# Attention, a rational-gate layer and four experts in one kernel: elementwise work of the front on GpSimd, another load order, and the last expert's products with the operands exchanged

## The chip, the cores and the metric

The kernel runs on one core of a Trainium2 chip. Five engines work side by side, each in the order of its own instructions: TensorE (PE, with its weight loads as PEld), VectorE (DVE), ScalarE (ACT), GpSimd (POOL) and SyncE (SP), which here only issues transfers. They wait for each other by semaphores. The metric is device time in microseconds (us); a smaller time is better.

## The reference, cut to what matters

Three layers follow each other. All is float32; NB = 4 batches, NH = 8 heads, S = 768 steps, D = 48.

```python
# 1: gated linear attention, per batch and head
f = 1 / (1 + exp(-f_logit))
state = f[t] * state + outer(k[t], v[t]);  y[t] = q[t] @ state
# 2: x: (3072, 384) from y;  w_in (384, 2048), w_out (2048, 384)
h = x @ w_in
g = (a0 + a1*h + a2*h**2 + a3*h**3) / (1 + |b0|*|h| + |b1|*h**2 + 1e-6)
x = g @ w_out
# 3: four experts, F = 1024
p = domain_probs / (domain_probs.sum(-1) + 1e-9)
out += p[:, e:e+1] * (relu(x @ w1[e]) @ w2[e])
```

## The kernel before

**Tiling.** The 768 steps are cut into six chunks of 128 steps (`c`), and a chunk holds the four batches' tokens side by side: 4 x 128 = 512 tokens. In a chunk the attention is made by block `(c, b)`, one for a batch. A block loads `f`, `k`, `q` (`Block.load`, 256 KB each) and `v` (`load_v`, 320 KB), takes `exp` and 1 + exp (`w`), multiplies along the steps by four scans (`scans`, result `g`), takes 1/g by logarithm, exponential and one Newton step (`inverse`, `newton1`, `newton2`), scales k by g (`k_hat`) and q by 1/g (`q_hat`), and then needs TensorE for the scores (`scores`), the transposed k (`k_t`, copied out by `k_copy`), the masked product with v (`masked`, `intra`) and the state's update (`update`, `finish`). `x_hi` copies the block's rows to x.

**The front.** Chunk 0 has nothing beside it. `Att.first(s, ...)` is called for s = 0 to 4 and writes out by hand the work of block s (`new`), block s - 1 (`old`) and the exponential of block s + 1 (`nxt`). In the same calls the weights of layer 2 come in as 64-bit numbers (`fetch`: two transfers of 768 KB, `raw`) and are turned into float32 by `conv(i, stage)`: two ScalarE instructions, a shift and a bit operation on VectorE, and one integer addition; the result `wf` is stored to DRAM (`w1s`). `conv` 0 falls into s = 1, 1 into s = 2, 2 and 3 into s = 3. In this kernel the addition of 0 to 3 and `k_hat` and `q_hat` of chunk 0 are VectorE's, the addition of 4 to 15 and `k_hat` and `q_hat` of later chunks GpSimd's. `warm` issues small products that nothing needs. The first product of layer 2 (`fill_in`, L880) waits for `x_hi` of block 3. Behind it come 6 chunks of layers 2 and 3, woven with the attention of the next chunk.

**The steady part.** Matrices and inputs of the later products are split into a high and a low part (`float32r`, one pass over TensorE), and each product is three: high by high, low by high, high by low. `mm_in` gives a 128 x 512 tile of h (nine instructions), `relu` its two parts, `mm_out` adds to three accumulators of 128 x 512 (nine instructions; rows are model columns, columns tokens). Products of chunk 0 in layer 2 are plain float32 (L880, L887), which takes two instructions each.

**The end.** When an expert is done, `evac2` multiplies the accumulators by the tokens' probabilities, spread over the rows (`pb`), and GpSimd adds them to `o`. For the last expert of the last chunk `end` does it on VectorE in six pairs of instructions, and then `write_out` turns `o` by twelve transposes on TensorE, copies by ScalarE and stores.

**Transfers.** SP issues nearly all transfers, in the order of the program. The program has eight semaphores for them, used in turn, so that the issue of a transfer waits until the one eight places before it (ScalarE's four first ones counted) has landed. It also waits until its target buffer is free: `f`, `k`, `q` and `v` have two buffers each.

Of the kernel before, what the change touches and what calls it, by code (L numbers as in the profile page):

```python
# [19 lines left out]
C = 128  # L20
# [379 lines left out]
class Block:  # L400
# [42 lines left out]
    def k_hat(self):  # L443
        k = self.k[0:PR]
        eng = self.nc.gpsimd if self.c else self.nc.vector
        eng.tensor_tensor(out=k, in0=k, in1=self.g[0:PR], op=ALU.mult)

# [10 lines left out]
    def q_hat(self):  # L458
        q = self.q[0:PR]
        eng = self.nc.gpsimd if self.c else self.nc.vector  # L460
        eng.tensor_tensor(out=q, in0=q, in1=self.i[0:PR], op=ALU.mult)

# [90 lines left out]
class Att:  # L553
# [24 lines left out]
    def start(self, fetch):  # L578
        nc = self.tc.nc
        for b in range(NB):  # L580
            nc.gpsimd.memset(self.st[b], 0.0)
        for b in range(2):
            blk = self.blocks[0, b] = Block(self, 0, b)
            for i in (2, 1, 0):
                blk.load(i)
            blk.load_v()
        for _ in range(3):
            fetch()

# [5 lines left out]

    def first(self, s, conv):

        new, old, nxt = (self.blocks.get((0, b)) for b in (s, s - 1, s + 1))
        rs = range(NP)
        if s == 0:  # L600
            new.exp()
            self.warm(WARM[0])
        if old:
            old.k_copy()
        if new:
            new.w()
            new.scans()
            new.inverse()
            new.k_hat()
        if nxt:  # L610
            nxt.exp()
# [29 lines left out]
        if old and s + 1 < NB:  # L641
            self.blocks[0, s + 1].load_v()

    def loads(self, v):
# [44 lines left out]
def fused(ctx, tc, aps, consts, gm, big, dp, prep, flag_op):  # L689
# [7 lines left out]
    banks = [pp.tile([128, 512], F32, name=f"bank{i}") for i in range(8)]  # L697
    acc, hb, h1 = banks[0:3], banks[3:5], banks[5]

    def pool(name, bufs):  # L700
# [27 lines left out]
    def conv(i, stage):  # L728
# [11 lines left out]
        else:  # L740
            nc.vector.tensor_scalar(pi, pi, 3, None, ALU.logical_shift_left)
            nc.vector.scalar_tensor_tensor(out=pi, in0=hi, scalar=-2 ** 31, in1=pi, op0=ALU.bitwise_and, op1=ALU.bitwise_or)
            w1f[i] = wp.tile([128, SW], F32, tag="w", name="wf")
            eng = nc.vector if CONV1[i] < NB - 6 else nc.gpsimd
            eng.tensor_tensor(out=w1f[i].bitcast(I32), in0=pi, in1=m, op=ALU.add)
            late.append(partial(nc.sync.dma_start, out=w1s[i], in_=w1f[i]))
# [99 lines left out]
    def mm_out(pairs, start, stop):  # L846
        for m in range(3):
            o = slice(m * 128, (m + 1) * 128)
            n, last = 0, 3 * len(pairs) - 1
            for (wh, wl), (gh, gl) in pairs:  # L850
                for a, b in ((wh, gh), (wl, gh), (wh, gl)):
                    nc.tensor.matmul(acc[m], a[:, o], b, start=(start and n == 0), stop=(stop and n == last))  # L852
                    n += 1
                    fill_step()

    def run_bounds(v):

        return (v % NJ2 == 0 or v in groups), ((v + 1) % NJ2 == 0 or v + 1 in groups)

    def emit(item):  # L860
# [9 lines left out]
        elif kind == "out2":  # L870
            mm_out([(ts[0], act2.pop(what))], *run_bounds(what))
        else:
# [137 lines left out]
    def write_out(c, b, bank):  # L1010
        for m in range(3):
            nc.tensor.transpose(bank[:, m * C:(m + 1) * C], o[c][:, m, b * C:(b + 1) * C], ident)
        if c < NCH - 1:
            t = osp.tile([128, DM], F32, tag="os", name="os")
        else:
            if b == 0:
                last.append(sp.tile([128, 3, 512], F32, tag="s1", name="os"))
            t = last[0].rearrange("p m t -> p (m t)")[:, b * DM:(b + 1) * DM]
        nc.scalar.copy(out=t, in_=bank[:, 0:DM])
# [14 lines left out]
    for v in range(-FILL - 6, LAST + 1):  # L1034
# [4 lines left out]
        if tau + 6 <= NB:  # L1039
            att.first(tau + 6, conv_ops(tau) if tau + 6 < NB else [[], []])  # L1040
        run_late()
# [254 lines left out]
```

## Time and profile before

| | us |
|---|---|
| median of 3 runs | 1397.06 (1396.53 to 1398.14) |
| the profiled execution, whole | 1395.27 |
| its span, first to last instruction | 1393.5 |
| PE, DVE, ACT, POOL busy | 1335.1, 889.1, 665.3, 290.5 |

The profile is one execution. What it shows lies in its span; some 1.8 us around it belong to the execution too. Busy shares are means over a front (up to 54 us), in which TensorE waits for the others, a long middle part, in which they wait for TensorE, and an end of some ten microseconds.

### The profile page before, as it was taken

Reading aid. Unit: us, or ns where it says so; the run is one execution under the profiler, and the core shown is the slowest. Engines: PE = TensorE matmul, PEld = TensorE weight load, DVE = VectorE, ACT = ScalarE, POOL = GpSimd, SP = SyncE. Lnnn points to the kernel's source line nnn. Section 1 sums busy time; section 2 is a strip of 40 time slices with the busy share of each in tenths; the row PEclk is TensorE's granted clock in tenths of the full one; section 3 lists DMA queues with packets and bytes.
Section 4 is the critical chain, followed back from the end, with each engine's and each line's share of the span. In section 5 each row is a group of like instructions: output and inputs, shape, how many; then the busy total and the mean of one; then the engine's idle time right before and its main releaser. Section 6 shows DMA issues by size and latency. Waiting matters only on the chain.

```text
span 1393.5 us, 19540 instructions
## 1 busy us (share of the span) xinstructions
PE 1335.1 (96%) x7134; PEld 1060.5 (76%) x7134; DVE 889.1 (64%) x1375; ACT 665.3 (48%) x1152; POOL 290.5 (21%) x257
## 2 busy tenths in 40 slices
PE   4799999899899999999999999999999999999997
PEld 4544787677678888877888877888888888888886
DVE  5899747697947666757666676566675556552222
ACT  3688437676626535534554435454454453431111
POOL 0133554566530010112001111001111001111010
PEclk8999999999999999999999999999999999999998
DMA  7546876667875656656755647566557566657660
GB/s 271 201 172 213 282 257 222 216 219 254 311 267 184 213 181 200 217 180 220 223 190 182 213 159 264 194 205 215 188 175 254 179 209 193 193 193 240 193 186 26
DMA packets 115704, 291.03 MB, mean 209 GB/s; under 512 B 13104, under 2 KB 28816, under 8 KB 114832
## 3 DMA queue, kind: packets, MB, share of 16 engines
q1 hardware_dynamic: 115024, 289.51, 62.8%
q8 instruction: 59, 0.97, 0.3%
q14 instruction: 45, 0.37, 0.1%
q10 hardware_dynamic: 576, 0.18, 0.1%
HBM read 240.83 MB, written 48.81 MB: 208 GB/s over the span
## 4 chain that ended last, share of the span: by engine, by line
PE 79%; DVE 13%; ACT 3%; DMA 2%; issue 1%; POOL 0%; SPq 0%; ACTq 0%; DVEq 0%; POOLq 0%
PE bank L852 36%; PE bank L842 33%; PE bank L887 3%; PE bank L880 3%; PE bank L489 2%; PE bank L465 1%; DVE q L916 1%; DVE g L435 1%; DMA f<-in_qkf_dram 1%; DVE q L925 1%; DVE y L935 1%; DVE y L937 1%; DVE q L911 1%; DVE q L913 1%; DVE gl L951 1%
## 5 line engine op out<-in xcount | busy, mean ns | idle before, releaser
L842 PE MATMUL bank<-x,w 128*128 128x512 f32 x2448 | 604.5, 394 | 11.3 <-DVE gl L951 9.1
L842 PEld LDWEIGHTS bank<-x,w 128*128 128x128 f32 x2448 | 457.3, 189 | 107.9 <-DVE gl L951 11.6
L852 PE MATMUL bank<-gh,w 128*128 128x512 f32 x1632 | 516.8, 396 | 6.6 <-DVE t L987 6.6
L852 PEld LDWEIGHTS bank<-gh,w 128*128 128x128 f32 x1632 | 302.8, 189 | 73.3 <-DVE t L987 7.4
L852 PE MATMUL bank<-gl,w 128*128 128x512 f32 x816 | 320.6, 393 | 0.0
L951 DVE SCALAR_TENSOR_TENSOR gl<-bank,gh 128x512 fp32r<-128x512 f32 x192 | 131.4, 685 | 153.0 <-ACT gh L950 152.5
L988 POOL TENSOR_TENSOR o<-o,t 128x512 f32<-128x512 f32 x69 | 89.0, 1319 | 549.4 <-DVE t L987 549.4
L852 PEld LDWEIGHTS bank<-gl,w 128*128 128x128 f32 x816 | 153.9, 189 | 33.1
L950 ACT ACTIVATE gh<-bank 128x512 fp32r<-128x512 f32 x192 | 113.6, 593 | 130.7 <-PE bank L842 130.7
L916 DVE SCALAR_TENSOR_TENSOR q<-q,sc,r 128x512 f32<-128x512 f32 x80 | 62.4, 780 | 152.3 <-ACT r L901 152.3
L799 POOL TENSOR_TENSOR w<-rawbuf,w 128x384 fp32r<-128x384 f32 x96 | 108.0, 1151 | 93.5 <-ACT w L798 77.5
L927 ACT CAST gh<-q 128x512 fp32r<-128x512 f32 x80 | 49.2, 615 | 159.0 <-DVE q L925 158.9
L896 ACT COPY h<-bank 128x512 f32<-128x512 f32 x80 | 46.8, 585 | 127.7 <-PE bank L842 127.2
L1005 DVE TENSOR_TENSOR s<-s,bank 128x512 f32<-128x512 f32 x45 | 30.6, 681 | 74.1 <-PE bank L852 74.1
L942 DVE TENSOR_TENSOR gl<-q,gh 128x512 fp32r<-128x512 f32 x80 | 56.0, 700 | 31.4 <-ACT gh L927 31.3
L917 ACT ACTIVATE r<-q,sc 128x512 f32<-128x512 f32 x80 | 58.0, 725 | 31.0 <-DVE q L916 24.2
L911 DVE SCALAR_TENSOR_TENSOR q<-q,r 128x512 f32<-128x512 f32 x80 | 65.7, 821 | 0.0
L902 ACT ACTIVATE y<-h,sc 128x512 f32<-128x512 f32 x80 | 64.2, 803 | 0.0
L435 DVE TENSOR_TENSOR_SCAN g<-f,sc 112x128 f32<-112x128 f32 x96 | 63.3, 719 | 0.5
L925 DVE SCALAR_TENSOR_TENSOR q<-y,sc,q 128x512 f32<-128x512 f32 x80 | 62.5, 781 | 1.8
L918 ACT ACTIVATE r<-r 128x512 f32<-128x512 f32 x96 | 60.8, 633 | 3.0
L937 DVE SCALAR_TENSOR_TENSOR y<-y,sc,h 128x512 f32<-128x512 f32 x80 | 60.1, 752 | 2.8
(103 smaller groups left out, 1216.4 us busy)
## 6 DMA issues: line engine op xcount, KB each, us to landing
w<-ws SPq DMA_DIRECT2D x448, 384.0 KB, 3.6
ws<-w SPq DMA_DIRECT2D x96, 384.0 KB, 4.0
raw<-in_w_dram SPq DMA_DIRECT2D x16, 768.0 KB, 6.9
rawbuf<-in_w_dram SPq DMA_DIRECT2D x64, 192.0 KB, 3.6
v<-in_v_dram SPq DMA_DIRECT2D x24, 320.0 KB, 4.7
f<-in_qkf_dram SPq DMA_DIRECT2D x24, 256.0 KB, 3.6
k<-in_qkf_dram SPq DMA_DIRECT2D x24, 256.0 KB, 4.1
q<-in_qkf_dram SPq DMA_DIRECT2D x24, 256.0 KB, 4.4
```

The costliest lines, as they stand in the source:

```text
L435: self.nc.vector.tensor_tensor_scan(g[:, r], f[:, r], lim, 1.0, ALU.mult, ALU.min)
L799: nc.gpsimd.tensor_tensor(out=t[:, 1], in0=r, in1=t[:, 0].bitcast(F32), op=ALU.subtract)
L842: nc.tensor.matmul(ps, a[:, o], b[:, kk, :], start=(n == 0), stop=(n == 8))
L852: nc.tensor.matmul(acc[m], a[:, o], b, start=(start and n == 0), stop=(stop and n == last))
L902: nc.scalar.activation(out=y, in_=h, func=AF.Identity, scale=sc[:, 0:1], bias=sc[:, 1:2])
L911: vec.scalar_tensor_tensor(out=q0, in0=q0, scalar=QC, in1=r0, op0=ALU.add, op1=ALU.mult)
L916: vec.scalar_tensor_tensor(out=q, in0=q, scalar=sc[:, 5:6], in1=r, op0=ALU.mult, op1=ALU.add)
L925: vec.scalar_tensor_tensor(out=q0, in0=y0, scalar=sc[:, 3:4], in1=q0, op0=ALU.subtract, op1=ALU.mult)
L937: vec.scalar_tensor_tensor(out=y, in0=y, scalar=sc[:, 2:3], in1=h, op0=ALU.subtract, op1=ALU.mult)
L950: nc.scalar.activation(out=gh, in_=h, func=AF.Relu)
L951: nc.vector.scalar_tensor_tensor(out=gl, in0=h, scalar=0.0, in1=gh.bitcast(F32), op0=ALU.max, op1=ALU.subtract)
L988: nc.gpsimd.tensor_tensor(out=o[c][:, m], in0=o[c][:, m], in1=t, op=ALU.add)
```

## The change

It has four parts. `k_hat` and `q_hat` of chunk 0 and the additions of `conv` 0 to 3 go from VectorE to GpSimd. Of the three pairs of `raw` loads that stood ahead of blocks 2 and 3 one stays; the second comes behind block 2's loads, the third behind block 3's and block 2's `v`. `k_copy` of the block before comes behind `inverse` on ScalarE. And the eight `mm_out` of the last expert of the last chunk become `mm_tokens`: the activations are the stationary operand, 128 tokens at a time, and the weights, 384 wide, move; four accumulators (`tok`) then hold tokens in rows. The sum of the other experts is transposed earlier, in the steps 4 and 3 before the last, and `end` has four VectorE instructions, each followed by its store.

```diff
     def k_hat(self):
-        eng = self.nc.gpsimd if self.c else self.nc.vector
-        eng.tensor_tensor(out=k, in0=k, in1=self.g[0:PR], op=ALU.mult)
+        self.nc.gpsimd.tensor_tensor(out=k, in0=k, in1=self.g[0:PR], op=ALU.mult)
...
     def q_hat(self):
-        eng = self.nc.gpsimd if self.c else self.nc.vector
-        eng.tensor_tensor(out=q, in0=q, in1=self.i[0:PR], op=ALU.mult)
+        self.nc.gpsimd.tensor_tensor(out=q, in0=q, in1=self.i[0:PR], op=ALU.mult)
...
-        for _ in range(3):
-            fetch()
+        fetch()
...
-        if old:
-            old.k_copy()
         if new:
             new.w()
             new.scans()
             new.inverse()
             new.k_hat()
+        if old:
+            old.k_copy()
...
             self.blocks[0, s + 1].load_v()
+        if s + 2 < NB:
+            fetch()
...
+    tok = acc + [h1]
...
-            eng = nc.vector if CONV1[i] < NB - 6 else nc.gpsimd
-            eng.tensor_tensor(out=w1f[i].bitcast(I32), in0=pi, in1=m, op=ALU.add)
+            nc.gpsimd.tensor_tensor(out=w1f[i].bitcast(I32), in0=pi, in1=m, op=ALU.add)
...
+    def mm_tokens(w, g, start, stop):
+        (wh, wl), (gh, gl) = w, g
+        for b in range(NB):
+            o = slice(b * C, (b + 1) * C)
+            for n, (a, m) in enumerate(((gh, wh), (gh, wl), (gl, wh))):
+                nc.tensor.matmul(tok[b][:, 0:DM], a[:, o], m, start=(start and n == 0), stop=(stop and n == 2))
...
     def end():
-        for h in range(2):
-            s = slice(256 * h, 256 * h + 256)
-            for m in range(3):
-                t = tp.tile([128, 512], F32, tag="t", name="t")
-                nc.vector.tensor_tensor(out=t[:, s], in0=acc[m][:, s], in1=pb[c][:, NE - 1, s], op=ALU.mult)
-                nc.vector.tensor_tensor(out=o[c][:, m, s], in0=o[c][:, m, s], in1=t[:, s], op=ALU.add)
-            for b in range(2 * h, 2 * h + 2):
-                write_out(c, b, banks[4 + b])
+        for b in range(NB):
+            t = last[0][:, b]
+            nc.vector.scalar_tensor_tensor(out=t, in0=tok[b][:, 0:DM], scalar=pn[:, c * NB + b, NE - 1:NE], in1=t,
+                                           op0=ALU.mult, op1=ALU.add)
+            nc.sync.dma_start(out=out[r0:r0 + C, :], in_=t)
...
+        if v in (LAST - 4, LAST - 3):
+            for b in range(2):
+                write_out(NCH - 1, b + 2 * (v - LAST + 4), banks[6 + b])
```

Where the change moves instructions, the order on the engines is this. First SP, from the loads of block 1 on to the `v` of block 2. Before:

```order
L420 DMA v<-in_v_dram 128x640
L726 DMA raw<-in_w_dram 128x1536 x6
L415 DMA f<-in_qkf_dram 128x512
L415 DMA k<-in_qkf_dram 128x512
L415 DMA q<-in_qkf_dram 128x512
L415 DMA f<-in_qkf_dram 128x512
```

And now:

```order
L420 DMA v<-in_v_dram 128x640
L726 DMA raw<-in_w_dram 128x1536 x2
L415 DMA f<-in_qkf_dram 128x512
L415 DMA k<-in_qkf_dram 128x512
L415 DMA q<-in_qkf_dram 128x512
L726 DMA raw<-in_w_dram 128x1536 x2
L415 DMA f<-in_qkf_dram 128x512
```

Block 2's `f` stood behind six `raw` transfers and stands behind two.

Then VectorE, from `newton2` of block 2 to the scans of block 3 (`i` is Newton's result, `t`, `raw` and `wf` belong to `conv` 1, `s` is the state, updated by `finish` of block 1). Before:

```order
L456 SCALAR_TENSOR_TENSOR i<-i,r 112x512
L461 TENSOR_TENSOR q<-q,i 112x512
L741 TENSOR_SCALAR t<-t 128x768
L742 SCALAR_TENSOR_TENSOR t<-raw,t 128x768
L745 ISA wf<-t 128x1536
L547 TENSOR_TENSOR s_1_140<-bank_92,i 48x4x48 x2
L428 TENSOR_SCALAR f<-f 112x512
L435 SCALAR_TENSOR_TENSOR g<-f,sc 112x128 x4
L446 TENSOR_TENSOR k<-k,g 112x512
```

And now (line numbers are those of the changed kernel):

```order
L455 SCALAR_TENSOR_TENSOR i<-i,r 112x512
L741 TENSOR_SCALAR t<-t 128x768
L742 SCALAR_TENSOR_TENSOR t<-raw,t 128x768
L545 TENSOR_TENSOR s_1_140<-bank_92,i 48x4x48 x2
L428 TENSOR_SCALAR f<-f 112x512
L435 SCALAR_TENSOR_TENSOR g<-f,sc 112x128 x4
```

`q_hat`, the addition and `k_hat` are gone from here; on GpSimd they now stand in the same order. The third place is the end of TensorE's work. Before, the last of the eight `mm_out` and the transposes behind it:

```order
L852 MATMUL bank_92<-gh,w 128x512 x2
L852 MATMUL bank_92<-gl,w 128x512
L852 MATMUL bank_93<-gh,w 128x512 x2
L852 MATMUL bank_93<-gl,w 128x512
L852 MATMUL bank_94<-gh,w 128x512 x2
L852 MATMUL bank_94<-gl,w 128x512
L1012 MATMUL bank_96<-ident,o 128x128 x3
L1012 MATMUL bank_97<-ident,o 128x128 x3
L1012 MATMUL bank_98<-ident,o 128x128 x3
L1012 MATMUL bank_99<-ident,o 128x128 x3
```

And now the place where six of the twelve transposes stand, between a `mm_in` (L841) and a `mm_tokens` (L860):

```order
L841 MATMUL bank_96<-x_10810,w 128x512 x9
L1020 MATMUL bank_98<-ident,o 128x128 x3
L1020 MATMUL bank_99<-ident,o 128x128 x3
L860 MATMUL bank_92<-w,gh 128x384 x2
L860 MATMUL bank_92<-w,gl 128x384
L860 MATMUL bank_93<-w,gh 128x384 x2
L860 MATMUL bank_93<-w,gl 128x384
L860 MATMUL bank_94<-w,gh 128x384 x2
L860 MATMUL bank_94<-w,gl 128x384
L860 MATMUL bank_97<-w,gh 128x384 x2
L860 MATMUL bank_97<-w,gl 128x384
```

Nothing follows the last `mm_tokens` on TensorE.

## Rows read from the trace of the kernel before

**Rows 1.** The page's head: busy us, share of the span, instructions.
```profile
PE 1335.1 (96%) x7134; PEld 1060.5 (76%) x7134; DVE 889.1 (64%) x1375; ACT 665.3 (48%) x1152; POOL 290.5 (21%) x257
```
**Rows 2.** The chain that ended last, in the front: start, length, what.
```profile
10.63 13.19 DMA f<-in_qkf_dram
...
50.80 1.30 DVE am L476 x2
...
54.18 2.62 PE bank L880 x6
```
**Rows 3.** Timeline of SP's issues: start, length, what.
```profile
6.80 3.71 SPq L726 DMA_DIRECT2D raw<-in_w_dram  x6
...
14.39 0.33 SPq L415 DMA_DIRECT2D f<-in_qkf_dram  x1
```
**Rows 4.** Three stretches: length, busy times, then granted clock, DMA share, GB/s.
```profile
0.00:12.00 12.00, 7.46 (x46) 7.34 (x48) 6.96 (x25) 3.90 (x6) 1.68 (x8) 1.00 0.85 295
12.00:16.00 4.00, 4.00 (x64) 3.56 (x60) 2.99 (x6) 1.69 (x3) 0.00 (x0) 1.00 1.01 421
44.00:48.00 4.00, 4.00 (x30) 3.74 (x28) 3.79 (x6) 2.10 (x5) 0.00 (x0) 0.57 0.52 207
```
**Rows 5.** Timeline of VectorE in the front.
```profile
25.37 0.56 DVE L741 TENSOR_SCALAR t<-t 128x768 int32<-128x768 int32 x1 [8.51 <-ACT t L738]
25.96 0.96 DVE L742 SCALAR_TENSOR_TENSOR t<-raw,t 128x768 int32<-128x768 int32 x1
27.07 0.96 DVE L745 CUSTOM_DVE_ANT_0 wf<-t 128x1536 uint16<-128x1536 uint16 x1
...
29.95 0.42 DVE L428 TENSOR_SCALAR f<-f 112x512 f32<-112x512 f32 x1
30.40 1.37 DVE L435 TENSOR_TENSOR_SCAN g<-f,sc 112x128 f32<-112x128 f32 x4
...
32.53 1.29 DVE L476 TENSOR_TENSOR am<-bank,mask 128x512 f32<-128x512 f32 x2
33.73 0.68 DVE L451 SCALAR_TENSOR_TENSOR i<-g,r 112x512 f32<-112x512 f32 x1
...
35.17 0.69 DVE L461 TENSOR_TENSOR q<-q,i 112x512 f32<-112x512 f32 x1
...
39.55 1.37 DVE L435 TENSOR_TENSOR_SCAN g<-f,sc 112x128 f32<-112x128 f32 x4
```
**Rows 6.** Groups of GpSimd, whole span: busy us, mean ns, idle before.
```profile
L446 POOL TENSOR_TENSOR k<-k,g 112x512 f32<-112x512 f32 x20 | 27.2, 1361 | 93.0 <-DVE g L435 88.8 <-DVE bank L920 3.8 <-POOL s L550 0.4
...
L745 POOL TENSOR_TENSOR wf<-t 128x768 int32<-128x768 int32 x12 | 21.8, 1819 | 96.4 <-DVE t L742 65.5 <-ACT y L902 10.6 <-ACT t L738 10.2
```
**Rows 7.** Timeline of VectorE where GpSimd scales chunk 1's k and q.
```profile
146.08 1.71 DVE L451 SCALAR_TENSOR_TENSOR i<-g,r 112x512 f32<-112x512 f32 x1 [0.92 <-ACT r L441]
...
156.91 1.25 DVE L476 TENSOR_TENSOR am<-bank,mask 128x512 f32<-128x512 f32 x2
```
**Rows 8.** Timeline of GpSimd in the same stretch.
```profile
145.96 1.28 POOL L446 TENSOR_TENSOR k<-k,g 112x512 f32<-112x512 f32 x1
...
157.07 1.30 POOL L446 TENSOR_TENSOR k<-k,g 112x512 f32<-112x512 f32 x1 [0.36 <-DVE g L435]
```
**Rows 9.** Timeline of the end: last product instruction and last store.
```profile
1382.52 0.40 PE L852 MATMUL bank<-gl,w 128*128 128x512 f32 x1
...
1388.21 0.44 SPq L1021 DMA_DIRECT2D out_dram<-os  x1
```
**Rows 10.** The chain that ended last, between experts of the middle part.
```profile
1256.96 2.04 PE bank L852 x9
1259.00 0.66 PE bank L1012 x6
```
**Rows 11.** A group of VectorE: 384 columns out of an accumulator bank.
```profile
L537 DVE TENSOR_TENSOR x<-bank,x 128x384 fp32r<-128x384 f32 x20 | 11.0, 548 | 0.0
```
**Rows 12.** The chain that ended last: six instructions of three plain float32 products.
```profile
74.28 2.58 PE bank L887 x6
```

More of the change, by code (lines that the diff above doesn't have):

```diff
@@ L594, in warm, with first @@
             self.tc.nc.tensor.matmul(self.spare[:, 0:C], ident, ident, start=True, stop=True)
-    def first(self, s, conv):
+    def first(self, s, conv, fetch):
         new, old, nxt = (self.blocks.get((0, b)) for b in (s, s - 1, s + 1))
@@ L854, in mm_out @@
                     fill_step()
+    def mm_tokens(w, g, start, stop):
[4 more added lines that the diff above has]
+                nc.tensor.matmul(tok[b][:, 0:DM], a[:, o], m, start=(start and n == 0), stop=(stop and n == 2))
+                fill_step()
     def run_bounds(v):
@@ L870, in emit @@
         elif kind == "out2":
-            mm_out([(ts[0], act2.pop(what))], *run_bounds(what))
+            if what >= LAST - NJ2:
+                mm_tokens(ts[0], act2.pop(what), *run_bounds(what))
+            else:
+                mm_out([(ts[0], act2.pop(what))], *run_bounds(what))
         else:
@@ L963, in end @@
         c = NCH - 1
-        for h in range(2):
-            s = slice(256 * h, 256 * h + 256)
-            for m in range(3):
-                t = tp.tile([128, 512], F32, tag="t", name="t")
-                nc.vector.tensor_tensor(out=t[:, s], in0=acc[m][:, s], in1=pb[c][:, NE - 1, s], op=ALU.mult)
-                nc.vector.tensor_tensor(out=o[c][:, m, s], in0=o[c][:, m, s], in1=t[:, s], op=ALU.add)
-            for b in range(2 * h, 2 * h + 2):
-                write_out(c, b, banks[4 + b])
+        for b in range(NB):
+            t = last[0][:, b]
+            nc.vector.scalar_tensor_tensor(out=t, in0=tok[b][:, 0:DM], scalar=pn[:, c * NB + b, NE - 1:NE], in1=t,
+                                           op0=ALU.mult, op1=ALU.add)
+            r0 = b * S + c * C
+            nc.sync.dma_start(out=out[r0:r0 + C, :], in_=t)
     def evac2(v):
@@ L1012, in write_out @@
             nc.tensor.transpose(bank[:, m * C:(m + 1) * C], o[c][:, m, b * C:(b + 1) * C], ident)
[L1013 to L1018, printed above, removed]
+        if c == NCH - 1:
+            if not last:
+                last.append(sp.tile([128, NB, DM], F32, tag="s1", name="os"))
+            nc.scalar.copy(out=last[0][:, b], in_=bank[:, 0:DM])
+            return
+        t = osp.tile([128, DM], F32, tag="os", name="os")
         nc.scalar.copy(out=t, in_=bank[:, 0:DM])
@@ L1039, in fused @@
         if tau + 6 <= NB:
-            att.first(tau + 6, conv_ops(tau) if tau + 6 < NB else [[], []])
+            att.first(tau + 6, conv_ops(tau) if tau + 6 < NB else [[], []], fetch)
         run_late()
```

## The prediction

> **What bounds the kernel now.** I read the head of the page first: TensorE is busy in 96% of the span [rows 1], so in the middle part every other engine is hidden behind it, and a gain must come from where TensorE waits. The chain that ended last says where. In the front it is a transfer: block 2's `f`, issued at 10.63, lands at 23.82 [rows 2]. From there the chain runs through VectorE to the `masked` of block 3 (50.80 to 52.10) and reaches the first product of layer 2 at 54.18 [rows 2]. The timeline of SP shows why `f` is late: six `raw` transfers of 768 KB stand ahead of it [rows 3]. VectorE's timeline shows its own share: additions of 0.96 each and k and q scalings stand in its row between the scans [rows 5]. From 54 us on the chain is nearly all products. In the end the last product instruction starts at 1382.52 and lasts 0.40, and the last store is issued only at 1388.21 [rows 9]: six pairs on VectorE, transposes and copies lie between.
>
> **The change part by part: load order.** `f` of block 2 now stands behind two `raw` transfers. Ahead of it and with it go blocks 0 and 1 (2 x 1088 KB), two `raw` (1536 KB), small constants (176 KB) and itself (256 KB), together 4.24 MB. By the rates of [rows 4] 3.54 MB are through at 12 us (295 GB/s) and the other 0.70 MB, at 421 GB/s, at 13.7. From the other side: before, `f` of block 3 needs the semaphore of the second `raw` and was issued at 14.39 [rows 3], so that `raw` had landed; 0.26 MB behind it end by 15.0. I take 14.4, 9.4 us earlier than 23.82. The first conversion's shift (L741) followed 1.55 later, at 25.37 [rows 5], so it could start at 15.9. But `q_hat` of block 1, now on GpSimd, runs from about 15.2 (`masked` of block 0 to 13.7, then Newton's step, which takes 1.44 from 33.73 to 35.17 [rows 5]) to 16.5, and I let L741 wait for it (why is below): 16.5. **Gain 8.9.**
>
> The transfers moved back keep cover: the second pair of `raw` is now issued at about 14, behind block 2's q, and lands near 19 (6.34 MB, 0.4 MB a us); `conv` 2 needs it at about 32. The third, behind `v` of block 2 at about 20, lands near 24 and is needed behind the first product. `f` of block 3 lands at 20 to 21 and is needed at 24. If a cover is gone, a pair costs 1.57 MB, 3.9 us.
>
> **Work to GpSimd.** From L741 on VectorE loses four additions (0.96 each) and two `k_hat` and two `q_hat` (the gap from the end of the scans at 31.77 to 32.53 holds one, 0.7 [rows 5]): 6.6 us. On GpSimd the same work takes 1.82 an addition and 1.27 to 1.36 a scaling [rows 6]. How much remains depends on whether the two engines run side by side. [rows 7] and [rows 8] show both answers. While GpSimd scaled k from 145.96 to 147.24, a VectorE instruction with two SBUF inputs, started at 146.08, took 1.71 instead of 0.68: it stood until GpSimd was nearly through (the 0.68 is the same instruction at 33.73 [rows 5]). But `masked`, which reads an accumulator and one SBUF tensor, took 1.25 beside a GpSimd scaling of 1.30, no more than the 1.29 of [rows 5]. So I let VectorE's scans, Newton steps, shifts and bit operations wait for a GpSimd instruction that has started, with 0.15 less than its length, and let `masked` and `finish` run. The Trainium skill says the same as a rule (SBUF — State Buffer, "SBUF: two separate sides"): the port pair that the two engines share is an exclusive lock, and whoever comes second, with two SBUF inputs on VectorE's side, blocks for the whole instruction. By that rule the front gains what I take; by the row of `masked` taken alone it would gain some 4 us more.
>
> In three stretches, from L741 at 16.5:
> - To the end of block 2's scans. Before 25.37 to 31.77, 6.4. Now shift and bit operation 1.56; addition on GpSimd 1.8, beneath it most of `finish` and `prep` (the 1.9 from 28.03 to 29.95 [rows 5]), of which 0.45 stays behind it; `w` 0.45; scans 1.4. Sum 5.7, so 22.2. Gain 0.7.
> - To the end of block 3's scans. Before 31.77 to 40.92, 9.15. Now `masked`, with `k_hat` and ScalarE's two steps beside it, 1.4; Newton 1.45; `q_hat` 1.2; shift and bit operation 1.56; addition 1.75, and `w` must wait for it; `w` and scans 1.85. Sum 9.2. Gain nothing (0.05 lost): what VectorE no longer works it waits.
> - To the end of block 3's `masked`. Before 40.92 to 52.10, 11.2. Now 1.4 + 1.45, shift 0.6, `q_hat` 1.2, bit operation 0.95, second shift 0.6, addition 1.7, second bit operation 0.95, `finish` 0.75, `masked` 1.3: 10.9; two of these overlap by some 0.2. Gain 0.5.
>
> **Gain 1.1** with these waits (the same sum done for the kernel before, on all engines, meets its first product within 0.2). Without them ScalarE's steps and TensorE fill the chain, and the gain of this part is 5.4: the other bound. From `masked` to the first product nothing changes. `k_copy` behind `inverse` costs nothing: `update` needs it only behind `masked` and `intra`, 1.3 and 1 us later. `q_hat`'s longer way to the scores hides too: TensorE is then still in block s - 1's `update` or VectorE not yet at `masked`.
>
> **The end.** The last copy's store was issued 5.3 behind the last product's end (1382.92 to 1388.21). Now one VectorE instruction from a bank, 384 wide (0.55 [rows 11]), with 0.1 on each side, lies between: 0.7. The three before it start while the products of later rows still run. **Gain 4.6.** Against it stand two costs on TensorE. Twelve transposes in the stream: six took 0.66 in the middle part [rows 10], so 1.3. Twelve products of 384 columns instead of nine of 512: nine take 2.04 [rows 10], 0.227 each; in proportion to columns twelve take 2.04 again. The kind does not occur, so bounds: nothing, or, if an instruction keeps its 0.227 whatever its width, 2.72 for twelve, eight times 0.68 = 5.4. The transposes, 128 wide and each with a weight load of its own, went by in 0.11 each, so neither the load nor the issue sets such a pace; I take 0.04 for each twelve, **0.3** in all, for gaps that stay as long per instruction. The end gains 3.0, between -2.1 and 3.3.
>
> **Sum.** 8.9 + 1.1 + 3.0 = 13.0 against the profiled execution's 1395.27: 1382.3. That execution lies 1.8 under the median of the runs shown; against 1397.06 the time is 1384.
>
> **The rivals.**
> 1. The engines do not hold each other up in the front (`masked` beside `k_hat` speaks for it, 1.71 against 0.68 speaks against it). Front 14.3, end 3.0: 1379.8.
> 2. The products pay for the front's gaps. TensorE now idles some 2.7 us before `intra` of block 3. Before, 44 to 48 us ran at a granted clock of 0.57, mostly 1.2 GHz, shortly behind an idle time of TensorE [rows 4]; if that falls on the first products, 3.5 us at half speed cost 1.8 to 3.5. With `f` landing 1 to 2 us late as well (behind 15 each us counts in full), and a part of the 5.4 at the end: 1386 to 1390, say 1387.
> 3. The gain moves: TensorE stands ready earlier, but a later wait (raw weights for `conv` 2 to 5, their stores on SP, which now stand behind GpSimd's additions) takes the front's 10 us. The 11 us of cover worked out above speak against it. Only the end remains: 1394.
> 4. Slower: 384-wide products with activations as the stationary operand do not run in one pass. Plain float32 takes 2.58 for three [rows 12], 0.86 each at 512 columns, 0.65 at 384; 96 of them cost 62 instead of 16.3, 46 more: 1430. The operands keep their type, which speaks against it. It decides from 0.14 more per product on (13.0 / 96).
>
> **How the numbers follow.** Chances: the forecast 0.62, rival 1 0.16, rival 2 0.14, rival 3 0.04, rival 4 0.04. The predicted time is the first one's, 1384. The range reaches from rival 1 with the end at its best (1379) to rival 2 with the clock and half of its delays (1389.5). What a measurement of this kernel can tell from no change is about 0.2%, 2.8 us: rivals 1, 2 and the forecast are all faster, rival 3 lies at the edge and is divided. Faster 0.94, same 0.02, slower 0.04.
>
> **What the profile after would show.** The exponential of block 2's `f` at 13.7 to 15; L741 first at 15.5 to 17; GpSimd's 1.82 additions with VectorE rows of 1 to 2 us where they were 0.4 to 0.96; the first product at 42.5 to 45.5; six transposes ahead of the fifth-last and of the fourth-last twelve products, and twelve in 2.0 to 2.3; the last store issued 0.6 to 0.9 behind the last product. I am wrong if the first product stands before 41 or behind 47, if the middle part's length (54 to 1350) differs by over 2 us, or if a 384-wide product shows more than 0.2 to the next.

## The result and the profile after

The changed kernel takes **1384.26 us** (median of 4 executions, 1383.59 to 1387.40), the kernel before 1397.60 beside it: ratio **0.9907** (95% interval 0.9894 to 0.9921). A second set of executions gave 1386.06 (1384.40 to 1386.67) against 1396.62, 0.9923 (0.9909 to 0.9936). The profiled execution takes 1383.59, its span 1381.6 (before 1395.27 and 1393.5).

The head of the page (busy us, share, instructions): VectorE's busy time, in which the time that an instruction is held up counts too, fell by 7 us, and GpSimd's rose by 18.

```profile
PE 1333.6 (97%) x7158; PEld 1062.6 (77%) x7158; DVE 881.9 (64%) x1355; ACT 664.8 (48%) x1152; POOL 308.4 (22%) x269
```

The chain that ended last, in the front (start, length, what), beside [rows 2]:

```profile
7.92 6.95 DMA f<-in_qkf_dram
...
40.95 1.30 DVE am L474 x2
...
43.45 1.74 PE bank L521 x8
45.19 3.38 PE bank L890 x6
...
58.01 2.81 PE bank L890 x6
```

Block 2's `f` lands at 14.9 instead of 23.8, `masked` of block 3 starts 9.85 earlier. Then 1.7 of it is lost: `update` (L521) takes 1.74 in the chain where it took 0.96, the first product 3.38 where it took 2.62, and the fourth product of layer 2 (58.01), from which on TensorE hardly waits, starts only 8.14 earlier than before (66.15). The windows view says why (the columns are those of [rows 4]): the granted clock of this stretch is 0.57, mostly 1.2 GHz, and TensorE is busy all of it. The clock fell at 43.2 and rose again at 46.6.

```profile
43.00:47.00 4.00, 4.00 (x27) 2.63 (x17) 1.69 (x4) 2.15 (x4) 0.00 (x0) 0.57 0.98 325
```

The kernel before had such a fall as well, but one block earlier: from 44.4 to 47.8, on the `update` (L523), the warming products (L594) and the scores (L465) behind block 2's `intra` (L489). TensorE's timeline before, from there to block 3's `intra`:

```profile
43.02 1.08 PE L489 MATMUL bank<-am,v 128*32 128x128 f32 x32 [1.75 <-DVE am L476]
44.03 1.54 PE L523 MATMUL bank<-v,kt 128*112 128x96 f32 x8
45.37 1.54 PE L594 MATMUL bank<-ident 128*128 128x128 f32 x6
46.84 1.59 PE L465 MATMUL bank<-q,k 48*128 48x128 f32 x16
...
52.14 1.08 PE L489 MATMUL bank<-am,v 128*32 128x128 f32 x32 [1.82 <-DVE am L476]
```

In the changed kernel TensorE stands still for 1.15 ahead of block 2's `intra`, no fall follows, and it stands still for 2.68 ahead of block 3's:

```profile
33.42 1.08 PE L487 MATMUL bank<-am,v 128*32 128x128 f32 x32 [1.15 <-DVE am L474]
34.43 1.02 PE L521 MATMUL bank<-v,kt 128*112 128x96 f32 x8
...
42.30 1.15 PE L487 MATMUL bank<-am,v 128*32 128x128 f32 x32 [2.68 <-DVE am L474]
```

The earlier fall cost nothing: between 41.7 and 50.8 the chain that ended last ran over VectorE, and TensorE waited for it afterwards all the same. The later one lies on the chain.

VectorE's timeline, beside [rows 5], and GpSimd's for the same time:

```profile
16.45 0.56 DVE L741 TENSOR_SCALAR t<-t 128x768 int32<-128x768 int32 x1 [1.64 <-ACT t L738]
...
18.67 0.25 DVE L1220 TENSOR_REDUCE pn<-pn 128x24 f32<-128x96 f32 x1
18.96 1.03 DVE L1221 TENSOR_SCALAR pn<-pn 128x24 f32<-128x24 f32 x1
...
22.71 1.29 DVE L474 TENSOR_TENSOR am<-bank,mask 128x512 f32<-128x512 f32 x2
...
25.95 1.39 DVE L741 TENSOR_SCALAR t<-t 128x768 int32<-128x768 int32 x1 [0.44 <-ACT t L738]
...
29.00 1.57 DVE L428 TENSOR_SCALAR f<-f 112x512 f32<-112x512 f32 x1
...
35.42 1.92 DVE L742 SCALAR_TENSOR_TENSOR t<-raw,t 128x768 int32<-128x768 int32 x1
...
37.84 2.45 DVE L742 SCALAR_TENSOR_TENSOR t<-raw,t 128x768 int32<-128x768 int32 x1
```
```profile
14.89 1.28 POOL L459 TENSOR_TENSOR q<-q,i 112x512 f32<-112x512 f32 x1 [1.56 <-DVE i L455]
18.15 1.81 POOL L744 TENSOR_TENSOR wf<-t 128x768 int32<-128x768 int32 x1 [1.98 <-DVE t L742]
22.91 1.27 POOL L445 TENSOR_TENSOR k<-k,g 112x512 f32<-112x512 f32 x1 [2.95 <-DVE g L435]
25.65 1.28 POOL L459 TENSOR_TENSOR q<-q,i 112x512 f32<-112x512 f32 x1 [1.47 <-issue]
28.48 1.80 POOL L744 TENSOR_TENSOR wf<-t 128x768 int32<-128x768 int32 x1 [1.55 <-DVE t L742]
...
35.01 1.51 POOL L459 TENSOR_TENSOR q<-q,i 112x512 f32<-112x512 f32 x1 [1.46 <-issue]
37.48 1.99 POOL L744 TENSOR_TENSOR wf<-t 128x768 int32<-128x768 int32 x1 [0.96 <-DVE t L742]
```

Each long VectorE row begins beside a GpSimd row and ends less than its own usual length behind that row's end: the shift at 25.95 (1.39 for 0.56) 0.41 behind `q_hat`, the `w` at 29.00 (1.57 for 0.42) 0.29 behind the addition, the bit operations at 35.42 and 37.84 (1.92 and 2.45 for 0.96) 0.82 behind the `q_hat` at 35.01 and the addition at 37.48. These two GpSimd rows began while a VectorE shift was running, and they are longer than usual themselves (1.51 for 1.28, 1.99 for 1.80). `masked` at 22.71, which reads an accumulator, takes its 1.29 beside `k_hat`.

The end, in the chain and in the timelines of TensorE and SP:

```profile
1351.34 2.10 PE bank L860 x12
1353.44 2.08 PE bank L841 x9
...
1359.71 0.66 PE bank L1020 x6
```
```profile
1375.32 0.34 PE L860 MATMUL bank<-w,gl 128*128 128x384 f32 x1
```
```profile
1376.35 0.37 SPq L979 DMA_DIRECT2D out_dram<-os  x1
```

The last store is issued 0.69 behind the last product's end; before it was 5.3 [rows 9]. Twelve products of 384 columns take 2.10, the nine of `mm_in` behind them 2.08 instead of 2.04 [rows 10], and six transposes 0.66 as in the middle part.

### The profile page after: what moved, and what is told of

Its sections match the earlier page's. It is cut to its first block, busy times and chain, and to the rows that moved or that the text cites. A ratio compares the mean times of both kernels' runs of the same rounds, so it can differ in the third digit from the quotient of the medians.

```text
span 1381.6 us, 19586 instructions
## 1 busy us (share of the span) xinstructions
PE 1333.6 (97%) x7158; PEld 1062.6 (77%) x7158; DVE 881.9 (64%) x1355; ACT 664.8 (48%) x1152; POOL 308.4 (22%) x269
## 4 chain that ended last, share of the span: by engine, by line
PE 79%; DVE 11%; ACT 3%; POOL 2%; DMA 2%; issue 2%; SPq 1%; ACTq 0%; POOLq 0%; DVEq 0%
PE bank L851 34%; PE bank L841 33%; PE bank L897 3%; PE bank L890 3%; PE bank L487 2%; POOL w L798 1%; PE bank L463 1%; DVE g L435 1%; PE bank L860 1%; DVE q L926 1%; DVE q L921 1%; DVE q L935 1%; DVE y L947 1%; DVE y L945 1%; DVE q L923 1%
## 5 line engine op out<-in xcount | busy, mean ns | idle before, releaser
L841 PE MATMUL bank<-x,w 128*128 128x512 f32 x2448 | 604.1, 394 | 9.7 <-DVE gl L961 7.5
L841 PEld LDWEIGHTS bank<-x,w 128*128 128x128 f32 x2448 | 457.2, 189 | 105.6 <-DVE gl L961 9.6
L851 PE MATMUL bank<-gh,w 128*128 128x512 f32 x1584 | 502.6, 397 | 6.6 <-DVE t L995 6.6
L851 PEld LDWEIGHTS bank<-gh,w 128*128 128x128 f32 x1584 | 294.2, 189 | 71.5 <-DVE t L995 7.5
L851 PE MATMUL bank<-gl,w 128*128 128x512 f32 x792 | 311.4, 393 | 0.0
L851 PEld LDWEIGHTS bank<-gl,w 128*128 128x128 f32 x792 | 149.5, 189 | 32.2
```

The lines of the kernel that those rows point to most:

```text
L841: nc.tensor.matmul(ps, a[:, o], b[:, kk, :], start=(n == 0), stop=(n == 8))
```

## The experiments

Every kernel was timed beside the kernel before. The table gives what its one profiled execution shows: when ScalarE starts on `f` of block 2, the first shift of `conv` 0, `masked` of block 3, the stretch between these two, TensorE's standstill ahead of `intra` of block 3, and the start of the fourth product of layer 2 with its distance from `masked`; then the median of all its executions and the ratio to the kernel before. The kernel before thus has a median for each set of kernels, and a ratio compares with that of the same set.

| kernel | f | shift | masked | stretch | standstill | 4th product | median | ratio |
|---|---|---|---|---|---|---|---|---|
| before | 23.84 | 25.37 | 50.80 | 25.43 | 1.82 | 66.15 (15.35) | 1396.6 to 1397.6 | |
| changed | 14.89 | 16.45 | 40.95 | 24.50 | 2.68 | 58.01 (17.06) | 1384.26 | 0.9907 |
| changed, again | 16.17 | 17.71 | 42.21 | 24.50 | 2.68 | 59.28 (17.07) | 1386.06 | 0.9923 |
| load order alone | 16.61 | 18.16 | 43.59 | 25.43 | 3.41 | 60.51 (16.92) | 1389.23 | 0.9946 |
| GpSimd alone | 23.43 | 24.96 | 49.46 | 24.50 | 2.68 | 66.52 (17.06) | 1395.57 | 0.9989 |
| end alone | 22.97 | 24.50 | 49.94 | 25.44 | 1.82 | 65.30 (15.36) | 1395.58 | 0.9987 |
| changed, without GpSimd | 14.57 | 16.14 | 41.58 | 25.44 | 1.83 | 56.95 (15.37) | 1387.20 | 0.9932 |
| part back on VectorE | 15.57 | 17.12 | 40.29 | 23.17 | 2.51 | 57.41 (17.12) | 1385.65 | 0.9907 |
| first gap filled | 15.78 | 17.32 | 41.84 | 24.52 | 0.45 | 57.28 (15.44) | 1384.33 | 0.9912 |
| both gaps, first try | 13.89 | 15.46 | 40.57 | 25.11 | 0.45 | 60.88 (20.31) | 1386.69 | 0.9928 |
| both gaps filled | 15.65 | 17.20 | 41.71 | 24.51 | 0.45 | 57.18 (15.47) | 1383.41 | 0.9906 |
| raw pair split | 13.68 | 15.27 | 41.46 | 26.19 | 2.68 | 58.52 (17.06) | 1383.32 | 0.9897 |
| split, part back | 13.53 | 15.30 | 38.46 | 23.16 | 2.51 | 53.90 (15.44) | 1381.41 | 0.9894 |
| split, part back, gaps filled | 13.52 | 15.30 | 38.47 | 23.17 | 0.27 | 53.92 (15.45) | 1380.16 | 0.9883 |

### The parts alone

**Load order alone.** The three edits of `fetch` in the kernel before.

```diff
-        for _ in range(3):
-            fetch()
+        fetch()
...
+        if s + 2 < NB:
+            fetch()
```

> The kernel before with the new load order alone; k and q scaling, additions and the end stay as they were. Theory (the load order is worth nearly all of the front's gain; the work given to GpSimd adds only 1.1 us at block 3's masked): f of block 2 lands at 14.9, first shift of conv 0 near 16.9 (ScalarE 1.5 behind the landing, q_hat of block 1 on VectorE), masked of block 3 at 42.1 instead of 50.80, first product near 45.4; the whole 8.5 to 9.4 us under the kernel before, that is 1386 to 1387 in the profiled execution. Rival (the two engines do not hold each other up, and GpSimd brings about 5 of the front's 9.9 us): masked of block 3 at 45 to 46, and only 4.5 to 5.5 us under the kernel before.

Measured 7.3 us under the kernel before (ratio 0.9931 to 0.9961). The first shift came 7.2 earlier and `masked` 7.2 earlier, not 8.7: `f` landed 1.7 later than in the changed kernel. The rest is the old stretch, 25.43. The profiled execution took 1389.44, where 1386 to 1387 was expected: the late `f` is 1.7 of that, and the clock, which fell here too, from 44.94 on, 1.6 (16.92 from `masked` to the fourth product for 15.35). The rival falls by its place, `masked` at 45 to 46: measured 43.59, with a later `f`.

```profile
43.59 1.30 DVE am L476 x2
44.88 0.04 issue
44.93 1.94 PE bank L489 x32
46.87 1.68 PE bank L523 x8
```

TensorE's timeline shows that block 2's part ran at full speed here, and that the standstill ahead of block 3's `intra` is then 3.41:

```profile
36.82 1.02 PE L523 MATMUL bank<-v,kt 128*112 128x96 f32 x8
37.68 0.86 PE L593 MATMUL bank<-ident 128*128 128x128 f32 x6
38.47 1.16 PE L465 MATMUL bank<-q,k 48*128 48x128 f32 x16
...
44.93 1.94 PE L489 MATMUL bank<-am,v 128*32 128x128 f32 x32 [3.41 <-DVE am L476]
```

These three rows took 3.04 here and 4.67 in the kernel before. The 1.63 between them is the difference between the two standstills (3.41 and 1.82) within 0.04, while VectorE's stretch is the same. So the short standstill of the kernel before was itself an effect of the clock fall on block 2's part.

**GpSimd alone.** `k_hat`, `q_hat`, the four additions and `k_copy` as in the change; load order and end as before.

```diff
-        eng = self.nc.gpsimd if self.c else self.nc.vector
-        eng.tensor_tensor(out=k, in0=k, in1=self.g[0:PR], op=ALU.mult)
+        self.nc.gpsimd.tensor_tensor(out=k, in0=k, in1=self.g[0:PR], op=ALU.mult)
...
-            eng = nc.vector if CONV1[i] < NB - 6 else nc.gpsimd
-            eng.tensor_tensor(out=w1f[i].bitcast(I32), in0=pi, in1=m, op=ALU.add)
+            nc.gpsimd.tensor_tensor(out=w1f[i].bitcast(I32), in0=pi, in1=m, op=ALU.add)
```

> The kernel before with k and q scaling of chunk 0 and the four additions on GpSimd and k_copy behind inverse; old load order, old end. Theory (VectorE waits while GpSimd runs): masked of block 3 at 49.3 to 50 instead of 50.80, VectorE rows of 1 to 2.5 us beside GpSimd's additions; the whole within 2 us of the kernel before on either side, because a clock fall on update and the first product can take 1.7 us back. Rival (no hold-up): masked of block 3 near 45.4, the whole 5 us under the kernel before.

The median is 1.0 lower (ratio 0.9978 to 0.9999). The stretch is 0.93 shorter and `f` came 0.4 earlier, but the clock's 1.71 takes back both: the fourth product starts 0.4 later than before. So the 1.0 doesn't come from the front: in the profile TensorE's time from the fourth product to the last one is 1.1 shorter, and why stays open. The rival (5 us) falls.

**End alone.** `mm_tokens`, the earlier transposes and the new `end` in the kernel before.

```diff
+            if what >= LAST - NJ2:
+                mm_tokens(ts[0], act2.pop(what), *run_bounds(what))
...
+        if v in (LAST - 4, LAST - 3):
+            for b in range(2):
+                write_out(NCH - 1, b + 2 * (v - LAST + 4), banks[6 + b])
```

> The kernel before with the new end alone (last expert's products with operands exchanged, earlier transposes, four instructions and stores at the end); the front stays as it was. Theory (the three gains add up, each in its own place): the last store is issued 0.7 behind the last product's end instead of 5.3; TensorE pays 2.0 more from the transposes of the middle on (1.32 for twelve transposes, 0.10 for each of eight pairs of mm_in and mm_tokens), so 2.7 us under the kernel before, near 1394 against 1396.6. Rival (part of the changed kernel's gain attributed to the front belongs to the end): 4 us or more under it; other rival (the end gave nothing): within 1 us.

Median 1.9 lower (ratio 0.9978 to 0.9997); the interval, 0.4 to 3.1 us, holds the expected 2.7, not 4, but by the times alone the end could have given under 1 us as well. The profile decides: the span ends 5.78 behind the last product's end instead of 10.58, a gain of 4.80; from the fourth product to the last product's end TensorE takes 1.95 more, which leaves 2.85.

**The changed kernel without GpSimd's part.** The reverse of the GpSimd edits, in the changed kernel; `k_copy` stays behind `inverse`.

```diff
-        self.nc.gpsimd.tensor_tensor(out=k, in0=k, in1=self.g[0:PR], op=ALU.mult)
+        eng = self.nc.gpsimd if self.c else self.nc.vector
+        eng.tensor_tensor(out=k, in0=k, in1=self.g[0:PR], op=ALU.mult)
...
-            nc.gpsimd.tensor_tensor(out=w1f[i].bitcast(I32), in0=pi, in1=m, op=ALU.add)
+            eng = nc.vector if CONV1[i] < NB - 6 else nc.gpsimd
+            eng.tensor_tensor(out=w1f[i].bitcast(I32), in0=pi, in1=m, op=ALU.add)
```

> The changed kernel with k and q scaling of chunk 0 and the additions of conv 0 to 3 back on VectorE; the new load order, k_copy behind inverse and the new end stay. Theory: masked of block 3 at 42.1, 1.2 later than in the changed kernel (40.95); the steady part starts 0.5 earlier to 1.2 us later than there (58.01), according to whether the clock falls on update and the first product here too; the whole 1383 to 1385 in the profiled execution against 1383.6. Rival (GpSimd works for nothing, side by side): masked of block 3 near 46, the whole 4 to 5 us slower than the changed kernel, 1388.

The stretch is 25.44, not 29: the rival's place, `masked` near 46, was missed by 4.4 us. With `k_copy` behind `inverse` the stretch is that of the kernel before (25.43), so that move cost nothing. The fourth product started 1.06 earlier than in the changed kernel: as in the kernel before, the clock fell one block earlier (35.0 to 38.4) and not on `update` and the first product. The profiled execution took 1384.51, as expected; the median of all, 1387.2, is 1 to 3 above the two sets of the changed kernel. The mean granted clock on record goes with it: 0.990 in the profiled execution, 0.987 in the four that took 1386.5 to 1388.2. As an estimate from these two numbers, 0.003 of 1383 us is some 4 us of TensorE's time. Where the clock fell in those four no trace shows.

### Does VectorE wait for GpSimd?

**Part back on VectorE.** `q_hat` of chunk 0 and the additions of `conv` 1 and 2 go back, `k_hat` and the additions of `conv` 0 and 3 stay.

```diff
-        self.nc.gpsimd.tensor_tensor(out=q, in0=q, in1=self.i[0:PR], op=ALU.mult)
+        eng = self.nc.gpsimd if self.c else self.nc.vector
+        eng.tensor_tensor(out=q, in0=q, in1=self.i[0:PR], op=ALU.mult)
...
-            nc.gpsimd.tensor_tensor(out=w1f[i].bitcast(I32), in0=pi, in1=m, op=ALU.add)
+            eng = nc.vector if i in (1, 2) else nc.gpsimd
+            eng.tensor_tensor(out=w1f[i].bitcast(I32), in0=pi, in1=m, op=ALU.add)
```

> The changed kernel with q_hat of chunk 0 and the additions of conv 1 and conv 2 back on VectorE; k_hat and the additions of conv 0 and 3 stay on GpSimd. Theory (VectorE stands for as long as GpSimd's instruction runs, unless it reads an accumulator bank): the shift of conv 1 and the bit operation of conv 2 lose holds of 0.83 and 0.96 and take back 0.69 each; the w of block 3 and the bit operation of conv 3 lose holds of 1.15 and 1.49 and take back 0.96 each; so the stretch from the first shift of conv 0 to masked of block 3 is 0.8 to 1.1 shorter than 24.50, at 23.4 to 23.7, although VectorE gets 3.3 us of work back. Rival (VectorE's own work sets the pace): the stretch is longer than 24.50, towards the 25.44 of the kernels with all of it on VectorE or beyond; whole time 0.5 to 1 us above the changed kernel.

The stretch is 23.17, 1.33 shorter (0.8 to 1.1 was expected), although VectorE got work back. Its timeline shows the holds gone:

```profile
26.82 0.55 DVE L742 TENSOR_SCALAR t<-t 128x768 int32<-128x768 int32 x1
...
30.14 0.43 DVE L428 TENSOR_SCALAR f<-f 112x512 f32<-112x512 f32 x1
...
36.11 0.96 DVE L743 SCALAR_TENSOR_TENSOR t<-raw,t 128x768 int32<-128x768 int32 x1
```

This settles that VectorE's own work alone doesn't set the pace: the holds count as well. All of the work on VectorE gives 25.43, all of it on GpSimd 24.50, and this division of it 23.17. The Trainium skill (SBUF — State Buffer, "SBUF: two separate sides") says that a VectorE instruction with two inputs in SBUF, or in a mode that uses both ports, and a GpSimd instruction make each other wait, for as long as the one that came first runs. The rows of the changed kernel agree where two inputs are read (1.92 and 2.45 for 0.96). The held shifts and the 24-wide TENSOR_SCALAR (1.03 for 0.18) have one input, and no row shows in which mode they ran. The whole didn't gain (1385.65): in the profiled execution the clock fell twice, at 42 to 46 and again at 56 to 64.

### What the clock costs

**First gap filled.** Ten more `warm` products behind those of block 3.

```diff
-            self.warm(WARM[2])
+            self.warm(WARM[2] + (10 if s == NB - 1 else 0))
```

> The changed kernel with ten more warming products (128 wide, results unused) behind those of block 3, in the gap in which TensorE stands still ahead of intra of block 3 (39.62 to 42.30). Theory (the standstill makes the clock fall from 43.2 to 46.5, on update of block 3 and the first product, and that costs 1.7 us): granted clock 1.00 there, update 1.0 instead of 1.81, the first product's six instructions 2.6 instead of 3.38, the steady part starts at 56.3 instead of 58.01; 1382 in the profiled execution. Rival (the fall has another cause, so it comes anyway, or the chain over ScalarE and VectorE behind the first product absorbs it): the steady part starts within 0.4 of 58.01, time unchanged at 1383.6.

`update` and the first product ran at full speed, and the fall came at the next standstill, on the fourth product:

```profile
44.20 1.02 PE L521 MATMUL bank<-v,kt 128*112 128x96 f32 x8
45.06 2.77 PE L890 MATMUL bank<-x,wf 128*128 128x512 f32 x6
...
57.28 4.51 PE L890 MATMUL bank<-x,wf 128*128 128x512 f32 x6 [3.11 <-DVE y L947]
```

4.51 instead of 2.81: the 1.7 was moved, not saved, and the median, 1384.33, lies between the two sets of the changed kernel. In the time the rival was right; in the place neither was, since filling the gap did keep the fall away from `update` and the first product, and it came behind the next gap.

**Both gaps, first try.** Besides the ten of the run before, three and twelve more ahead of the third and fourth products. The fifteen go into a bank that the gate layer uses; only the new line is shown.

```diff
+        att.warm({2: 3, 3: 12}.get(j, 0), banks[7])
```

> The changed kernel with the ten warming products ahead of intra of block 3 (as in the run before) and three and twelve more ahead of the third and fourth products of layer 2, where TensorE stood for 0.84 and 3.11 and where the clock fell instead. Theory (the fall follows a standstill of about 3 us in the front and is only moved by filling one of them): no fall behind 40 us, update of block 3 1.0, the four first products 2.8 each; 1.7 to 1.9 us under the changed kernel, 1382 against 1384. Rival (the fall comes anyway, later, in the middle part): granted clock 0.5 for 3.4 us at another place behind 61 us and time unchanged, 1384.

A failed experiment: the twelve waited 3.83 for the gate's use of that bank, filled nothing and ran mostly at half speed (the clock fell from 56.2 to 59.6) ahead of the product. Median 1386.69. Here `f` came early, at 13.89, and the first shift was held by `q_hat` (1.14 for 0.56), which is why the stretch, counted from the shift's start, is 25.11.

```profile
56.72 4.32 PE L591 MATMUL bank<-ident 128*128 128x128 f32 x24 [3.83 <-ACT bank L911]
```

**Both gaps, second try** ("both gaps filled" in the table). The ten stay, the three are left out, and the twelve go to `acc[0]`, which is free there.

```diff
+        att.warm(12 * (j == 3), acc[0])
```

> The changed kernel with the ten and twelve warming products alone. In the earlier run with fifteen behind the first products those were held up by the bank that they wrote to, which the gate layer uses, so the gap was not filled; here they write to an accumulator that is free. Theory: no fall behind 40 us; steady part starts at 56.3 (for a first shift at 16.45) instead of 58.01, 1.7 us under the changed kernel. Rival (it comes later all the same, on products of the middle part): a stretch of granted clock 0.5 behind 61 us, time unchanged.

No fall from 31 to 228 us, and the fourth product 15.47 behind `masked` instead of 17.06. Median 1383.41, 0.85 and 2.65 under the two sets of the changed kernel, the second of which ran beside it. So both halves of the expectation are met: 1.6 in the front, and no fall on the products right behind it.

### The load order, further

**Raw pair split.** The second transfer of the first pair goes behind block 2's q.

Here `fetch(0)` issues the first transfer of the pair, `fetch(1)` the second.

```diff
-        fetch()
+        fetch(0)
...
+        if s == 0:
+            fetch(1)
```

> The changed kernel with only the first raw transfer of the first pair ahead of f of block 2; the second one is issued behind q of block 2 (it is needed by conv 1, at 25). Theory (the landing of f sets the front, and it is set by the bytes ahead of it): 0.77 MB less ahead of f, which lands 1.5 to 2 us earlier, near 13; the first shift then comes as soon as Newton's step of block 1 is done and q_hat on GpSimd lets it, at 15.0 to 16.2 instead of 16.45; masked of block 3 earlier by as much, 0.3 to 1.4. Rival (f's landing is not set by the bytes ahead of it): it lands within 0.5 of 14.89, or later, and nothing moves.

`f` of block 2 was there by 13.68 (13.53 and 13.52 in the two later kernels with this split, 13.9 to 16.6 in the eight profiles without it), and the shift came at 15.27 (held to 1.32 by `q_hat`). But the stretch grew by 1.7: now `f` of block 3 is late, and ScalarE's conversion of `conv` 1 is queued behind its exponential.

```profile
25.73 0.63 ACT L424 ACTIVATE f<-f 112x512 f32<-112x512 f32 x1 [1.67 <-DMA f<-in_qkf_dram]
26.26 0.88 ACT L744 ACTIVATE t<-raw 128x768 f32<-128x768 f32 x1
```

The median is 0.9 under the first set of the changed kernel; the profiled execution was the longest of four (1386.65, mean granted clock 0.989; the others 1383.1 to 1383.6, 0.991), so how often `f` of block 3 is late isn't known.

**The changed kernel again**, unaltered.

> The changed kernel unaltered, as a reference on the same chip and as a second profile. Expected by the account so far: 24.50 from the first shift of conv 0 to masked of block 3 again (the order of the engines sets it), while the landing of f of block 2 and the place at which the clock falls can differ; 12 to 14 us under the kernel before. If instead the stretch itself differs by over 0.3, the comparisons of stretches between kernels are worth less than was taken.

The same stretch to the hundredth; `f` 1.3 later, and 1.8 more in the median. That is 10.6 under the kernel before, where 12 to 14 was expected; in the first set it was 13.3, so two sets of one kernel can lie 2.8 apart.

**Split, part back.** The split pair, `f` of block 3 ahead of the second pair, and "part back".

```diff
                 blk.load(i)
+                if s == 1 and i == 2:
+                    fetch()
```

> The changed kernel with q_hat of chunk 0 and the additions of conv 1 and 2 back on VectorE, the second raw transfer of the first pair behind q of block 2, and f of block 3 ahead of the second pair. Theory: f of block 2 lands before 13.7, first shift at 15.3 to 15.6, f of block 3 no longer late, so 23.2 from there to masked of block 3 (38.7 against 40.95); the clock may still fall on the first products; 2.0 to 2.5 us under the changed kernel. Rival (the stretch gets longer again because f of block 3, or the raw of conv 1 or 2, is late): stretch over 24, gain under 1 us.

38.46 and 23.16 as expected, no fall in this execution: 1381.41, ratio 0.9879 to 0.9909. That is 4.6 under the changed kernel of the same set, where 2.0 to 2.5 was expected with a fall still possible; without one the fourth product starts 5.4 earlier than in that profile (53.90 for 59.28).

**Split, part back, gaps filled.** The same with the warming products of the second try.

```diff
+            self.warm(WARM[2] + (10 if s == NB - 1 else 0))
...
+        att.warm(12 * (j == 3), acc[0])
```

> The same as the run before with ten more warming products ahead of intra of block 3 and twelve ahead of the fourth product of layer 2, these into an accumulator that nothing uses there. Theory (a fall needs a standstill of TensorE before it): no fall behind 40 us and 1.7 us under the run before, 3.7 to 4.2 under the changed kernel, 1380. Rival (the fall comes at another place and costs the same): time as in the run before.

**1380.16** (1379.92 to 1380.55), ratio 0.9883 (0.9867 to 0.9898), 5.9 under the changed kernel in the same set; all its executions are shorter than any of the changed kernel or of the kernel before. The windows view of the stretch in which the clock fell in the changed kernel shows 1.00 (third figure from the end), and TensorE busy in 3.73 and 4.00 of 4:

```profile
39.00:43.00 4.00, 3.73 (x48) 2.62 (x48) 1.83 (x5) 2.04 (x4) 0.76 (x1) 1.00 0.62 184
43.00:47.00 4.00, 4.00 (x11) 1.57 (x9) 2.46 (x4) 2.66 (x6) 1.81 (x1) 1.00 0.76 309
```

What the filled gaps add to the run before is not shown here. That run's profile had no fall to save, and the two fourth products start at the same time (53.90 and 53.92); of the 0.9 between the two profiled spans, 1.0 lies between the fourth product and the last one.

## Why the prediction was right, and where not

The time, 1384.0 for 1384.26, was right, and in part by luck. In spans the gain is 11.9 where 13.0 was summed: 9.85 to `masked`, less 1.71, plus 1.10 in the middle, plus 2.66 at the end. The 1.71 and the 1.10 were both not forecast and partly made up for each other. The medians lie 13.3 apart in the first set and 10.6 in the second, so the agreement to 0.3 us says little.

- **Load order, 8.9.** Measured 8.92 (25.37 to 16.45), though not for the reason given: `f` came 0.5 later than taken, and the shift followed 1.56 behind it, while `q_hat` happened to end just before. That two different waits end 0.3 apart is luck. The range for the landing, 13.7 to 15.0, was too narrow: with this load order ScalarE began on `f` at 13.9 to 16.6 in eight profiles.
- **GpSimd, 1.1.** Measured 0.93, in four kernels with all of this work on GpSimd (24.50 to 24.52) against four without (25.43 and 25.44). The parts were distributed otherwise: 0.2, -0.2 and 1.0 for the three stretches, where 0.7, 0 and 0.5 were forecast; the hold on `prep`'s TENSOR_SCALAR (0.85) was not counted. That the engines hold each other up, on which rival 1 was judged, is shown by the stretch that got shorter when work went back.
- **"From `masked` to the first product nothing changes."** This is the step that failed. To the first product it took 0.82 more (4.03 for 3.21), to the fourth 1.71: the clock part of rival 2, priced at 1.8 to 3.5 and given a chance of 0.14 together with a late `f`. That the clock costs this is shown: in the six profiles of the table with a fall here the fourth product comes 16.92 to 17.12 behind `masked`, in the seven without one 15.35 to 15.47 (the first try of both gaps, with its late twelve, left out). The forecast left the fall of the kernel before where it was; only rival 2 asked whether it could land on the first products. There it lay on block 2's part, where TensorE has time to spare, and now it lies on `update` and the first product, which are on the chain. It came there in one profile with a standstill of 3.41 ahead of `intra`, in five of six with 2.5 to 2.7, and in none of four where the gap was filled (three of the table and the first try). In the three with 1.8 the clock had fallen one block earlier, behind standstills of 1.75 to 2.03, so they don't show that a short standstill keeps a fall away. Why it comes at one block or at the other stays open.
- **The end, 4.6 less 1.6.** The first part is 4.64 (10.58 to 5.94 from the last product to the span's end). The cost is 1.98 from the last transposes of the middle part to the last product's end: the transposes 1.32 as forecast, but a pair of `mm_in` and `mm_tokens` takes 4.18 instead of 4.08: the twelve lose 0.06 where 0.04 was taken, and the nine behind them 0.04 where nothing was. Net 2.66 for 3.0.
- **The middle, 1.10, was not forecast and is not explained.** From the start of the fourth product to that of the last one, eight profiles with this middle and end, and no clock fall on the fourth product, take 1317.3 to 1319.3, so a difference of that size shows between single profiles without any change to this part.
- **Rivals.** 1 fell by the holds; 3 fell (8.14 of the front's 9.85 is still there at the fourth product; the 11 us of cover named for it are 13 by the prediction's own 19 and 32, which changes nothing); 4 fell: twelve products in 2.10, 0.17 to the next. The other signs came as named: first product at 44.98, VectorE rows of 1.0 to 2.5 beside GpSimd's.

## What to carry to other kernels

Here moving VectorE's work to GpSimd paid where VectorE meanwhile read an accumulator or waited anyway, and lost where the two held each other up; look at which instruction stands beside each moved one, not at the sum of busy time. When a front gets shorter, look for the half-speed stretches that it already had and ask where they will lie afterwards: the one that lay behind VectorE's work cost nothing here, the one on the chain 1.6 to 1.7 us, and filling one gap may only move it to the next. A transfer issued earlier has a landing time with a spread; plan for what becomes late next.

## What had not been expected of the hardware

- The price of a clock fall between `masked` and the first product is nearly the same in all kernels where it came, 1.6 to 1.7. Yet neither the length of the standstill nor its place decides alone: at 2.51 it came in one profile and not in another, behind the standstill ahead of block 2's `intra` it came at 1.75 (the kernel before), 1.85 (changed, without GpSimd) and 2.03 (end alone), and ahead of the fourth product, with 3.1 to 3.2, only in two of the eleven profiles that have this gap. What decides in such cases stays open.
- A single-input TENSOR_REDUCE ran beside GpSimd's addition in its usual 0.25 (18.67), while the TENSOR_SCALAR behind it, on 24 numbers a row, stood until the addition was over.
- Within a group, products of 384 columns come 0.173 apart for the most part and products of 512 columns 0.227. The 128 columns more cost 0.053, that is 0.417 ns a column, one cycle at 2.4 GHz; at this rate 0.013 is left over at either width.
